# Inner seven-product multiplications for two of the seven up products of a mixture-of-experts kernel

## The chip, the cores and the metric

The kernel runs on one core of a Trainium2 chip. The metric is the device time of one execution in microseconds (us); lower is better. Before the change three runs took 1023.96, 1022.22 and 1023.16 us, a median of 1023.16.

## What is computed

Attention with feature maps makes x, of 4608 rows and 512 columns. Then every one of 8 experts is applied to all rows, and the results are added with weights P that come from a gate by eight rounds of row and column normalisation. Only the second part is touched:

```python
N, D, E, F = (4608, 512, 8, 1024)
...
for e in range(E):
    h = np.maximum(x @ w1[e], 0.0)
    ye = h @ w2[e]
    out += P[:, e:e + 1] * ye
```

## The kernel before

**Tiles.** The 4608 rows are 9 groups g of 512 rows. `xT` in SBUF holds x transposed, 512 features on four blocks of 128 partitions. Expert 0 runs on plain matmuls (L581) while the attention and the routing still use the other engines. Experts 1 to 7 use a multiplication of 2x2 blocks with seven products in place of eight (Strassen in Winograd's form): `sums_up` (L1201) makes sums of the blocks of w1 on VectorE, `sums_down` (L1226) those of w2, and `sums_x` (L1277) sums of the blocks of x, once, in expert 1; they are stored in DRAM (`Xd`) and loaded again by `load_x` (L1295) for each later expert.

**Stages.** Groups are worked in pairs (0,1), (2,3), (4,5), (6,7), and group 8 alone. For a pair there are two calls of `up7` (L1321), one for each half `fp` of the 1024 hidden columns; for group 8 there is one. Each call stands in one stage together with one `down7` (L1441) for one earlier group. So an expert has 4 x 2 + 1 = 9 stages, and the seven experts have 63. In experts 1 to 6 group 8 comes last, in expert 7 first.

**The up products.** In a pair's stage `up7` makes the seven products for two tiles q of 128 hidden columns. Each product for one q is two 512-column matmuls (`wide`, L1312, recorded at L1316), one for each 128 rows of its K of 256. So a stage has 7 x 2 x 2 = 28 of these. Their names are x1 (a block of w1 times a block of x, both as they are: product "11"), y1, x2, w1 (product "s1": a sum of w1 blocks times a sum of x blocks), x3, x4 and w2; x10 is x1 for q = 0. x1, x2, x3 and x4 add up in one PSUM bank per q. After x1, x2 and x3 ScalarE copies this running sum into an SBUF buffer U (`keep`, L1359), and VectorE adds U to the bank of y1, w1 or w2, clips at zero and writes the hidden tile `hs` (`add`, L1363, recorded at L1364). After x4 ScalarE applies Relu to the bank (`relu`, L1368).

**The down products.** `down7` has seven products X1, Y1, Z1, X2, X3, Z2, X4, each of eight 256-column matmuls (`product`, L1301, recorded at L1307), 56 in a stage. VectorE makes sums of the hidden tiles first (`sub`, L1199, 128x512 each). A product's bank is read into the accumulator `acc` either by VectorE (`read`, L1501) or, in `read2` (L1507), by two ScalarE reads scaled by P (L1513) and a POOL addition (L1516). Each of X1 and Y1 has such a `read2` into the same part of `acc`.

**Order.** All operations are recorded in a `Plan` (L192) first. A list scheduler with its own durations for each engine then writes them out: it always takes the operation that can start first, and among equals the one recorded first. For a stage, the order of recording is the string `ORDER` (L1566). PSUM has eight banks of 512 fp32 columns per partition, which `Banks` (L70) hands out one or two at a time. The rings T (sums of w1, 4 buffers), U (4) and X (sums of x, 4) are handed out in the same way. `sub` operations and POOL's operations are planned as sharing one port.

## Time and profile before

| | |
|---|---|
| median of three runs | 1023.16 us |
| span of the profiled execution, first to last instruction | 1020.7 us (no other time of this execution is given; the median lies 2.46 above it) |
| granted TensorE clock | 1.000 of full speed |
| matmul L1316, 128x512, and L1307, 128x256 | 379 ns and 273 ns each |
| ScalarE copy into U, L1360, 128x512 | 588 ns, x378 |
| ScalarE scaled read, L1513, 128x256 | 476 ns, x496 |
| ScalarE Relu, L1369, 128x512 | 609 ns, x126 |
| VectorE addition with clipping, L1364, 128x512 | 687 ns, x378 |
| POOL addition, L1516, 128x512 | 1309 ns, x248 |

The engines are PE (TensorE's matmuls), PEld (its weight loads), DVE (VectorE), ACT (ScalarE), POOL (GpSimd) and SP (which issues DMAs). A group's mean is the length of one instruction from its start to its end. Instructions of one engine overlap: of two that follow each other without a wait, the second starts before the first ends. So the time by which one instruction moves the next, its pace, is shorter than its length, and is read from rows of the timeline that merge several of them.

### The profile page before, as it was taken

What the parts mean: (1) busy time and instruction counts of PE and PEld (TensorE: products, weight loads), DVE (VectorE), ACT (ScalarE), POOL (GpSimd) and SP (SyncE); (2) the same over time, 40 slices, a digit from 0 to 9 for tenths busy, and PEclk for the clock granted to TensorE, in tenths of its full rate; (3) what the DMA queues carried; (4) which work ended last, traced back from release to release, by engine and by line L of the source; (5) the groups of instructions that cost most, each with busy time, mean ns of one, the idle gap of its engine ahead of it and who ended that gap; (6) DMA issues with size and microseconds to landing.
All of it is one profiled execution on the core that took longest, in us unless ns stands there. A gap on an engine that the chain in (4) does not pass through costs nothing.

```text
span 1020.7 us, 21372 instructions
## 1 busy us (share of the span) xinstructions
PE 1007.1 (99%) x7944; PEld 686.1 (67%) x7944; DVE 853.2 (84%) x1833; ACT 701.6 (69%) x1530; POOL 466.8 (46%) x480
## 2 busy tenths in 40 slices
PE   7899999999999999999999999999999999999998
PEld 5666666644566766676667766676667666776665
DVE  7999989987888987788778887788778877888776
ACT  7999999836778665666666666556666666655663
POOL 5778764400244444444444444544444444544443
PEclk9999999999999999999999999999999999999999
DMA  9999988160103311161106111421125110612333
GB/s 264 174 194 175 174 149 126 36 114 11 42 32 69 82 32 32 27 135 32 32 27 114 33 42 37 82 54 32 31 47 115 32 32 26 109 43 73 129 124 130
DMA packets 107016, 82.86 MB, mean 81 GB/s; under 512 B 53536, under 2 KB 89376, under 8 KB 106912
## 3 DMA queue, kind: packets, MB, share of 16 engines
q1 hardware_dynamic: 74960, 57.44, 22.4%
q0 software_dynamic: 31648, 23.86, 16.9%
q8 instruction: 62, 1.02, 0.4%
q14 instruction: 42, 0.34, 0.1%
q10 hardware_dynamic: 304, 0.20, 0.1%
HBM read 83.18 MB, written 12.98 MB: 94 GB/s over the span
## 4 chain that ended last, share of the span: by engine, by line
PE 95%; ACT 2%; DVE 1%; issue 0%; POOL 0%; DMA 0%; DVEq 0%; ACTq 0%
PE ps L1307 41%; PE ps L1316 33%; PE ps L581 18%; PE ps L864 2%; PE ps L711 0%; ACT q L577 0%; DVE m L573 0%; ACT k L577 0%; DVE wx L573 0%; DMA acc<-in_k_dram 0%; PE ps L893 0%; ACT kr L577 0%; ACT wx L577 0%; DVE xb L878 0%; PE ps L903 0%
## 5 line engine op out<-in xcount | busy, mean ns | idle before, releaser
L1516 POOL TENSOR_TENSOR acc<-acc,hx 128x512 f32<-128x512 f32 x248 | 322.9, 1309 | 476.7 <-ACT hx L1513 473.3
L1360 ACT COPY U<-ps 128x512 f32<-128x512 f32 x378 | 216.6, 588 | 134.1 <-PE ps L1316 117.6
L1513 ACT ACTIVATE hx<-ps,P 128x256 f32<-128x256 f32 x496 | 208.0, 476 | 124.6 <-PE ps L1307 112.0
L1364 DVE CUSTOM_DVE_ANT_0 hs<-ps,U 128x512 bf16<-128x512 f32 x378 | 253.0, 687 | 35.7 <-PE ps L1316 15.0
L1307 PEld LDWEIGHTS <-hs 128*128 128x128 bf16 x1984 | 194.1, 98 | 72.8 <-issue 0.2
L1501 DVE SCALAR_TENSOR_TENSOR acc<-ps,P,acc 128x256 f32<-128x256 f32 x372 | 161.2, 478 | 92.3 <-PE ps L1307 91.5
L1307 PEld LDWEIGHTS <-hx 128*128 128x128 bf16 x1488 | 145.6, 98 | 40.0 <-issue 0.2
L1307 PE MATMUL ps<-hx,hs 128*128 128x256 bf16 x992 | 132.5, 273 | 0.0
L1316 PE MATMUL ps<-X,T 128*128 128x512 bf16 x448 | 129.0, 379 | 0.3 <-ACT U L1360 0.2
L1316 PE MATMUL ps<-xT,wx 128*128 128x512 bf16 x384 | 101.5, 379 | 0.0
L1316 PEld LDWEIGHTS <-T 128*128 128x128 bf16 x672 | 65.8, 98 | 48.0 <-issue 0.3
L1369 ACT ACTIVATE hs<-ps 128x512 bf16<-128x512 f32 x126 | 73.2, 609 | 12.3 <-PE ps L1316 12.3
L1307 PE MATMUL ps<-wx,hs 128*128 128x256 bf16 x560 | 80.4, 273 | 0.0
L1316 PEld LDWEIGHTS <-wx 128*128 128x128 bf16 x512 | 50.1, 98 | 38.4 <-issue 0.5
L1316 PE MATMUL ps<-xT,w 128*128 128x512 bf16 x288 | 75.6, 379 | 0.0
L581 PE MATMUL ps<-w,hx 128*128 128x512 bf16 x288 | 73.7, 379 | 0.0
L581 PE MATMUL ps<-xT,w 128*128 128x512 bf16 x288 | 72.9, 379 | 0.0
L1307 PE MATMUL ps<-wx,hx 128*128 128x256 bf16 x496 | 68.4, 273 | 0.0
L1316 PE MATMUL ps<-xT,T 128*128 128x512 bf16 x224 | 66.0, 379 | 0.0
L1307 PE MATMUL ps<-hx 128*128 128x256 bf16 x496 | 64.3, 273 | 0.1
L1199 DVE TENSOR_TENSOR hx<-hx,hs 128x512 bf16<-128x512 bf16 x124 | 64.2, 518 | 0.0
L1307 PE MATMUL ps<-w,hs 128*128 128x256 bf16 x432 | 62.7, 273 | 0.0
(147 smaller groups left out, 1516.2 us busy)
## 6 DMA issues: line engine op xcount, KB each, us to landing
X<-xd SPq DMA_DIRECT2D x72, 256.0 KB, 2.6
wx<-in_moe_w_dram POOLq DMA_DIRECT2D x8, 1024.0 KB, 12.5
v_m<-in_v_dram SPq DMA_DIRECT2D x15, 512.0 KB, 5.3
out_dram<-acc SPq DMA_DIRECT2D x14, 512.0 KB, 2.8
w<-in_moe_w_dram POOLq DMA_DIRECT2D x6, 1024.0 KB, 12.0
qk<-in_k_dram POOLq DMA_DIRECT2D x12, 256.0 KB, 5.5
qk<-in_q_dram POOLq DMA_DIRECT2D x12, 256.0 KB, 6.3
xd<-X SPq DMA_DIRECT2D x12, 256.0 KB, 2.1
```

The lines of the kernel that those rows point to most:

```text
L581: nc.tensor.matmul(out_, lhsT=lhsT, rhs=rhs, start=start, stop=stop)
L864: pe(65, lambda j=j: nc.tensor.matmul(pn()[:, j * D1:j * D1 + D1], lhsT=s["T"][x]()[:, j % 2, 2 * h + j // 2, :] if j < 4 else r["T"][x]() ...
L1199: lambda: f.tensor_tensor(out=out_(), in0=x(), in1=y(), op=op), r, w, **kw)
L1307: pe(256, lambda i=i, k=k, z=z: nc.tensor.matmul(bank()[:, 256 * i:256 * i + 256], lhsT=lhs(k, i), rhs=rhs(k), start=first and z, stop=k = ...
L1316: pe(512, lambda k=k: nc.tensor.matmul(bank().rearrange("p (a b) -> p a b", a=2), lhsT=lhs(k), rhs=rhs(k), start=first and k == 0, stop=k ...
L1360: act(512, lambda: nc.scalar.copy(out=u[q][n]().rearrange("p a b -> p (a b)"), in_=x[q]()), [x[q]], [u[q][n]])
L1364: dve(515, lambda: nc.vector._custom_dve(ADD_SAT, out=out_(q, i, j), in0=bank[q]().rearrange("p (a b) -> p a b", a=2), in1=u[q][n](), s0=3 ...
L1369: act(512, lambda: nc.scalar.activation(out=out_(q, i, j), in_=x[q]().rearrange("p (a b) -> p a b", a=2), func=ACT.Relu, bias=0.0, scale=1 ...
L1501: dve(320, lambda n=n, ts=ts: nc.vector.scalar_tensor_tensor(out=acc[g][:, ts, 256 * j:256 * j + 256], in0=bank()[:, 256 * n:256 * n + 256 ...
L1513: act(370, lambda n=n: nc.scalar.activation(out=u()[:, n, :], in_=bank()[:, 256 * n:256 * n + 256], func=ACT.Copy, bias=0.0, scale=P[:, 4 ...
L1516: pool(695, lambda: nc.gpsimd.tensor_tensor(out=acc[g][:, 2 * i:2 * i + 2, 256 * j:256 * j + 256], in0=acc[g][:, 2 * i:2 * i + 2, 256 * j: ...
```

## The change

Four things change together.

- **Inner products.** In experts 2 to 7, for pairs of groups, the products "11" (x1) and "s1" (w1) are no longer four 512-column matmuls each for the two q. Each becomes seven products of half the size again, a chain of seven 256-column matmuls with K = 128, named ia1 to ia7 (for "11") and ib1 to ib7 (for "s1"). The running sums of these chains stay in PSUM: after the first product ScalarE copies half a bank into half of another bank, after the second it copies half a bank into a U buffer, and after the third and the fourth VectorE adds U and writes half a bank of PSUM. The fifth to seventh products then accumulate on these halves. `inner_sums` makes the four sums of w1 blocks for each chain in T (for expert 7 in the free w1 buffer). `inner_x` makes sums of x blocks during expert 1, three of which go to DRAM through a new ring XI of two buffers and are loaded for every pair of the later experts; the fourth overwrites a block of xT.
- **Running sums copied between banks.** In all seven experts, where x1's sum went into U and VectorE added it to y1's bank, ScalarE now copies it into y1's bank (`move`), y1 accumulates on it, and ScalarE applies Relu. x2's sum is copied in the same way into a bank for w2. w1's sum is kept in U and added at x3. So per q there are two additions by VectorE and two Relus in place of three and one. In `down7`, X1's sum is copied into Y1's bank by ScalarE, and only Y1 is read into `acc`.
- **Banks.** A bank on which matmuls accumulate after a copy (kind "onto") must have been written over its whole width before; `Banks` keeps the set `whole` of those.
- **Rings and order.** T has 5 buffers, U 3, X 3, XI 2. Stages with inner products are recorded in the new order `INNER`.

```diff
-    ring("s_p", [128, 1024], BF16, "T", 4)
-    ring("s_p", [128, 2, 256], FP32, "U", 4)
-    ring("s_p", [128, 2, 2, 256], BF16, "X", 4)
+    ring("s_p", [128, 1024], BF16, "T", 5)
+    ring("s_p", [128, 2, 256], FP32, "U", 3)
+    ring("s_p", [128, 2, 2, 256], BF16, "X", 3)
+    ring("s_p", [128, 3, 256], BF16, "XI", 2)
...
+    def inner_sums(w1, i, key, late, spare, at):
+        S = spare or new("T")
...
+        for n, x, y, op in ((3, b(0, 0), b(1, 0), ALU.subtract), (1, b(1, 0), b(1, 1), ALU.add),
+                            (2, c(1), b(0, 0), ALU.subtract), (4, b(0, 1), c(2), ALU.subtract)):
+            sub(dve, 256, c(n), x, y, op, k + late, [own])
...
+    def inner_x(gs, r0=()):
+        keys = xall(gs)
+        for n, j in INNER_X:
+            X = {n: new("XI")}
+            b = [[xpart(gs, j, k, a) for a in range(2)] for k in range(2)]
...
+            sub(dve, 256, t(3), b[1][1], b[0][1], ALU.subtract, keys + ["late", *r0], w)
+            sub(dve, 256, b[0][1], b[0][1], b[0][0], ALU.subtract, ["late", *r0], keys)
+            sub(dve, 256, t(2), b[1][1], b[0][1], ALU.subtract, keys + ["late", *r0], w)
+            sub(dve, 256, t(4), b[1][0], t(2), ALU.subtract, keys + ["late", *r0], w)
+            move_x(gs, n, True, X)
...
+        def move(to, q):
+            act(512, lambda: nc.scalar.copy(out=to[q](), in_=x[q]()), bk(x[q]), [to[q]])
...
+        def chain(name, o, r, takes, wk, posts):
...
+            def step(i):
+                if i == 1:
+                    one(1, 0, "11", "11", True)
+                    copy(at(0, 0), 0, k[0, 0])
+                elif i == 2:
+                    one(1, 1, "s1", "t1")
+                    copy(s, 1, (p5, n))
+                elif i == 3:
+                    one(1, 0, "s2", "t2")
+                    plus(0, 1)
+                elif i == 4:
+                    one(1, 0, "s3", "t3")
+                    plus(1, 1)
+                elif i == 5:
+                    one(0, 0, "12", "21")
+                elif i == 6:
+                    one(0, 1, "s4", "22")
+                    posts(0)
+                else:
+                    one(1, 0, "22", "t4")
+                    posts(1)
...
         def x1(q):
-            prod(x, q, "11", "11", True, more, u[q] + hb)
-            keep(q, 0)
+            prod(x, q, "11", "11", True, more, hb)
+            move(y, q)
 
         def y1(q):
-            prod(y, q, "12", "21", True, r0, hb)
-            add(y, q, 0, 1, 1)
+            prod(y, q, "12", "21", False, r0, hb)
+            relu(y, q, 1, 1)
 
         def x2(q):
             prod(x, q, "s2", "t2", False)
-            keep(q, 1)
+            move(z, q)
 
         def w1(q):
-            prod(w, q, "s1", "t1", True, A["s4"][1] + r0, hb, [("banks", q)])
+            prod(w, q, "s1", "t1", True, A["s4"][1] + r0, hb, [("banks", 0, q)])
+            keep(q)
 
         def x3(q):
             prod(x, q, "s3", "t3", False)
-            keep(q, 0)
-            add(w, q, 0, 0, 0)
+            add(x, q, 0, 0)
...
         def w2(q):
-            prod(w, q, "s4", "22", False)
-            add(w, q, 1, 1, 0)
+            prod(z, q, "s4", "22", False)
+            add(z, q, 1, 0)
...
         def X1():
             prod(x, a(0, 0), "11", hk(0, 0), True, sk(1) + hk(1, 0),
                  [("D", e, g)])
-            read2(x, 0, 0)
+            act(512, lambda: nc.scalar.copy(out=y(), in_=x()), [x], [y])
 
         def Y1():
-            prod(y, a(0, 1), "21", hk(0, 1), True, [("D", e, g)])
+            prod(y, a(0, 1), "21", hk(0, 1), False, [("D", e, g)])
             read2(y, 0, 0)
...
+    INNER = ("ib1 ia1 ia2 ib2 ib3 ia3 X1 Z1 ib5 ia4 ib4 ia5 ia6 ib6 y10 X2 x20 ia7 X3 x21 ib7 "
+        "x31 y11 w20 x30 Z2 x40 x41 Y1 X4 w21").split()
```

In the chain, `one(i, h, ...)` is the 256-column matmul into half h of bank i (bank 0 is the chain's result for q = 0, bank 1 for q = 1), `copy` is a 256-column ScalarE copy, `plus` a 256-column VectorE addition into PSUM, and `posts` is what followed x1 or w1 before: `move` into y's bank for "11", `keep` into U for "s1".

## The prediction

> **What bounds the kernel now.** I read the page's engine shares first, then the chain that ended last, then the busy time in windows inside the experts.

> ```profile
> span 1020.7 us, 21372 instructions
> ...
> PE 1007.1 (99%) x7944; PEld 686.1 (67%) x7944; DVE 853.2 (84%) x1833; ACT 701.6 (69%) x1530; POOL 466.8 (46%) x480
> ...
> PE 95%; ACT 2%; DVE 1%; issue 0%; POOL 0%; DMA 0%; DVEq 0%; ACTq 0%
> PE ps L1307 41%; PE ps L1316 33%; PE ps L581 18%; PE ps L864 2%; PE ps L711 0%; ACT q L577 0%; DVE m L573 0%; ACT k L577 0%; DVE wx L573 0%; DMA acc<-in_k_dram 0%; PE ps L893 0%; ACT kr L577 0%; ACT wx L577 0%; DVE xb L878 0%; PE ps L903 0%
> ```

> TensorE is busy for 99% of the span, and 95% of the last chain lies on it, 74% in L1307 and L1316, the products of experts 1 to 7. The window over the middle (columns: window, length, then busy us and count of PE, weight loads, DVE, ACT, POOL, then the granted clock, DMA share, GB/s):

> ```profile
> 514.00:621.00 107.00, 107.00 (x770) 75.06 (x768) 87.53 (x183) 66.24 (x140) 47.89 (x38) 1.00 0.24 54
> ```

> TensorE has no idle time here, at clock 1.00. Work taken off it is time won, and each wait put on it is time lost; nothing else can be won there. The chain in order of time shows one piece, 13.97 us of L1307, at 332.96, 442.51, 551.99, 661.47 and 770.95: 109.5 us for an expert, 12.17 for each of its 9 stages. That fixes the unit of what follows.

> **What leaves TensorE.** The timeline gives the pace of matmuls (start, us, engine, line, operation, shapes, count):

> ```profile
> 548.37 1.03 PE L1316 MATMUL ps<-X,T 128*128 128x512 bf16 x4
> ...
> 551.83 1.04 PE L1307 MATMUL ps<-hx,hs 128*128 128x256 bf16 x8
> ```

> One 512-wide matmul lasts 0.379 us in the groups, so the next starts (1.03 - 0.379)/3 = 0.217 later; I use 0.216. For 256 wide it is (1.04 - 0.273)/7 = 0.1095. A stage of 28 wide and 56 narrow ones is 28 x 0.216 + 56 x 0.1095 = 12.18, as measured. In each of the 48 changed stages (6 experts, 4 pairs, 2 halves) 8 wide ones become 14 narrow ones: 1.728 us become 1.533, so 0.195 less. **48 x 0.195 = 9.4 us.** The build agrees: 384 wide matmuls fewer, 672 narrow ones more. Their weight loads double per column, but L1307 keeps this pace with a 0.098 us load for each 0.1095 us matmul, so loads stay covered. Up to the last products of expert 0 the order on TensorE is the same; expert 1 has the same matmuls as before.

> **What is added on other engines, all beside TensorE.** ScalarE: of a stage's six 512-wide copies into U, four now write PSUM, at the same count; two Relus are added (0.52 each from pairs of L1369), four 256-wide copies in a changed stage, and in the down product one 512 copy (0.485, from pairs of L1360 that take 1.07) replaces two scaled reads (0.42 each). From 66.24/107 x 12.17 = 7.53 us per stage this makes 7.53 + 1.04 + 4 x 0.31 + 0.485 - 0.84 = 9.5 of 11.98. VectorE: two additions of L1364 leave (0.60 each), four 256-wide additions into PSUM come, and the sums of weights. L872 is their nearest row, VectorE from PSUM to PSUM with 325 elements at 495 ns, and TensorE accumulates on it afterwards; at L1364's slope (512 elements, 687 ns) 256 elements take about 0.42, paced 0.33. From 87.53/107 x 12.17 = 9.95 this makes 9.95 - 1.20 + 1.32 + 0.28 (eight weight sums over eight stages) = 10.35 of 11.98. POOL loses one 1.31 us addition a stage. The 48 weight sums (256 elements; 0.285 from the rows of 512 at 0.418 and 1024 at 0.685) and 32 sums of x are 23 us of VectorE, hidden under TensorE unless they stand in front of something it waits for (below). XI adds 8 stores and 48 loads of 192 KB on SP; each load is asked for when the previous pair's seventh inner product is done (4 to 5 us into its second stage) and needed 1.3 us or more into the next stage, 8 us later. X loads land in 2.6 us by the median and 7.3 at most. X with three buffers reloads each a stage ahead of use. I cost all of it at nothing; a pair whose load came without that cover would wait up to 2.6 us.

> **What waits are added.** Here lies the risk: each inner chain has three round trips, TensorE to ScalarE or VectorE and back, and what waits on TensorE holds everything behind it. I followed the build's order through a pair's two stages and through a change of expert, with three allowances. A narrow result is ready 0.20 us after the next matmul could start: 0.273 - 0.1095, and 0.04 until its reader starts (two matmuls end at 545.05, L1360 starts at 545.09). From an end to the waiting matmul I take 0.06 (L872 ends at 35.92, its matmul starts at 35.98). The rest are the paces above; times below count from the stage's first inner product. The tightest place is the start of a pair's second stage: the first products of both chains are readable at 0.53 us, and four 256 copies follow each other. No ScalarE write to PSUM and no plain 256 copy is in the trace. Nearest rows, both from PSUM to SBUF:

> ```profile
> 102.11 1.24 ACT L577 ACTIVATE kr<-ps 128x256 bf16<-128x256 f32 x4
> ```

> ```profile
> 548.20 0.84 ACT L1513 ACTIVATE hx<-ps,P 128x256 f32<-128x256 f32 x2 [0.47 <-PE ps L1307]
> ```

> Four Exps take 1.24 us, a pace of 0.27. The scaled copy paces 0.364 and lasts 0.476; it reads a scale per partition, which the new copy does not. By the first row the third and fourth copies end at 1.50 and 1.77 and TensorE may go on at 1.56 and 1.83; it arrives at the two third products at 1.64 and 1.86. No wait. By the second row they end at 1.73 and 2.10: 0.30 us lost by the fourth. I take the first, since like the new copy it reads no memory scale, and keep the second as an end. The next tightest there is ia7: VectorE has an addition at 2.31, subtractions at 2.66 and 3.04, and the addition that ia7 waits for from 3.45 to 3.87; go at 3.93, reached at 3.96. The other products have 0.03 to 0.1 to spare; nothing is late. In a pair's first stage two are late. Z1's bank is read until 1.05, go at 1.11, reached at 1.09: 0.02. For ib5 VectorE has w21's addition at 0.97, a subtraction at 1.57 and the addition from 1.90 to 2.33; go at 2.39, reached at 2.32: 0.07. After a change of expert five T buffers are refilled, the last four weight sums just before ib1; the build fills in with some 27 down matmuls, and only w20 is late (ScalarE's Relu at 4.87, the copy from 5.40 to 5.99, go at 6.05, reached at 6.00). That is 0 in half of the stages and 0.09 in the other half: 48 x 0.045 = **2.2 us lost**. The other end, the scaled copy's row in 24 second stages, is 24 x 0.30 = 7.2 more; below zero nothing is possible, since TensorE has no idle to give back.

> [...]

> **Sum.** The profiled execution spans 1020.7; the median of 1023.16 lies 2.46 above it, which I keep as what lies around the span (no other time of that execution is given). 1020.7 - 9.4 + 2.2 = 1013.5, and 1013.5 + 2.46 = **1016.0**.

> **Rivals.**
> 1. *The copies into PSUM are slower than the Exps.* For it: no row shows the operation, and ScalarE goes from 62% to 80% busy. Against: pace 0.27 of the nearest row. At L1513's price 1016.0 + 7.2 = 1023.2, no change; halfway about 1019.6.
> 2. *VectorE's queue becomes the bound, and it ends slower.* Fourth and seventh products wait for a 256 addition, and in the build a pair's second stage puts two L1199 subtractions right before one of them, with 0.03 to spare. L1199 can be held up by POOL:

> ```profile
> 547.81 2.68 POOL L1516 TENSOR_TENSOR acc<-acc,hx 128x512 f32<-128x512 f32 x2 [3.08 <-ACT hx L1513]
> ...
> 548.01 1.34 DVE L1199 TENSOR_TENSOR hx<-hx,hs 128x512 bf16<-128x512 bf16 x1
> ```

> 1.34 us in place of 0.42. Over all four forms the means are 518, 439, 421 and 418 ns: 124 x 124 ns = 15.4 us of such delay, 0.25 a stage. If it falls before an addition in every changed stage: 48 x 0.25 = 12 us, 1028.0. It decides from 9.4/48 = 0.196 us of waits per stage. Against: POOL has a quarter less to do, and in my walk the subtractions end before POOL starts.
> 3. *The change does not shorten TensorE's work*, because narrow matmuls pace at their weight loads. The L1307 row excludes it.

> **How the numbers follow.** A measurement of this kernel tells about 0.2% (2 us) from no change: 1021.1 to 1025.2 is "the same". The forecast, 1013 to 1019, has 0.62. Rival 1 has 0.21, spread over 1019 to 1025, 0.11 of it below 1021.1. Rival 2 has 0.13, 1025 to 1034, with 0.01 on the side of the same. Faster than 1013 or anything unnamed: 0.04, of which 0.02 is faster. So faster 0.75, the same 0.12, slower 0.13 (0.01 of the unnamed). The floor is the full gain, 1020.7 - 9.5 + 2.46 = 1013.7, less 0.9 for the spread of the three runs: 1012.8. Upwards, 1022.5 leaves out rival 2, the top of rival 1 and half of the unnamed, 0.19 in all.

> **What would show it.** TensorE's busy time falls to about 998 us. An expert from 2 to 6 takes 109.5 - 8 x 0.15 = 108.3 us. The 256 copies' pace is near 0.27, the 256 additions last near 0.42, and TensorE's waits for ScalarE and VectorE inside the experts total 1 to 4 us; if they are over 9 us, rival 1 or 2 holds, and the line named in the wait tells which. L1199's mean falls from 518. XI never appears as a releaser. I am wrong if a bank, a T buffer or XI, and not a copy or an addition, holds TensorE.

## The result and the profile after

The changed kernel takes **1027.68 us** (median of four runs, 1026.86 to 1029.21) against 1023.28 in the same comparison: a ratio of 1.0048 [1.0034, 1.0062]. It is slower, by about 0.5%; 1016.0 was forecast, in a range up to 1022.5. The profiled span went from 1020.7 to 1025.3, +4.6.

The page of the changed kernel, first lines and the chain that ended last:

```profile
span 1025.3 us, 22492 instructions
...
PE 1001.4 (98%) x8232; PEld 712.2 (69%) x8232; DVE 849.4 (83%) x1979; ACT 799.8 (78%) x1786; POOL 385.7 (38%) x418
...
PE 91%; DVE 5%; ACT 3%; DMA 1%; issue 1%; SPq 0%; DVEq 0%; ACTq 0%
```

TensorE is busy for 5.7 us less, but idle for 23.9 us where it was 13.6; VectorE's share of the last chain rose from 1% to 5%. The window over the middle, same columns as before:

```profile
514.00:621.00 107.00, 106.25 (x815) 79.43 (x814) 87.95 (x207) 81.25 (x181) 36.44 (x29) 1.00 0.31 69
```

VectorE's load is hardly other than before (87.53), POOL's fell from 47.89 to 36.44, the clock is 1.00. The same piece of an expert in the chain in order of time gives the length of an expert:

```profile
558.50 15.50 PE ps L1379 x142
...
667.84 15.50 PE ps L1379 x142
...
777.28 15.50 PE ps L1379 x142
```

109.34 and 109.44 us, before 109.5; 108.3 was forecast. What holds TensorE between 260 and 1010 us is in the view of its waits (who waited <- for whom: us, times, longest):

```profile
PE ps L1475 <- DVE ps L1487: 5.3, 8, 0.8
PE ps L1379 <- ACT hx L1656: 1.6, 2, 1.2
PE ps L1388 <- DVE hs L1450: 1.6, 3, 1.2
PE ps L1388 <- DMA X<-xd: 1.2, 1, 1.2
```

In the kernel before this view has one line, 0.2 us. It counts only idle time; a wait also takes the 0.16 us by which one narrow matmul otherwise starts before the other's end. So I also add up, over all pairs of successive matmuls, the time from start to start less the pace (0.216 us, narrow 0.1095). This **lateness** is the measure in the rest; the line numbers of after are L1475 (inner products), L1484 (their copies), L1487 (their additions), L1447 (copies between banks), L1450 (addition with clipping), L1211 (all sums), L1659 (POOL's addition).

| kernel | 255 to 340 us (expert 1) | 340 to 925 | 925 to the end | sum |
|---|---|---|---|---|
| before | 0.4 | -0.9 | -0.2 | -0.7 |
| after | 3.4 | 8.3 | 1.7 | 13.4 |

The sum of before is the error of the two paces. The difference, 14.1 us, less the 9.4 us by which the narrow matmuls are shorter, is 4.7: the span's 4.6. So the gain is there in full, and 14.1 us of waits stand against the 2.2 that were forecast. By place:

- **A, 4.6 us.** Five times 0.92 us, at 379.60, 489.02, 598.11, 707.63 and 816.89: the fifth inner product of a chain (ib5) waits for an addition, where the down products change from one expert to the next.
- **B, 3.0 us more than before in expert 1**, where the up products are those of before: waits of 1.36 and 0.60 for ScalarE, and one of 1.34 for VectorE (an x4, see runs 3 and 4).
- **C, 2.5 us** in the first inner products of expert 2 (354 to 360 us): five waits, three of them, 2.1 us, for additions (0.43, 0.79 and 0.84).
- **D, 1.4 us** in expert 7: X is not there.
- **The rest, 2.6 us**, in many waits of 0.4 us and less.

A, then the last two waits of C, then D in the timeline of after (start, length, engine, line, operation, then idle time and what ended it):

```profile
485.36 1.34 POOL L1659 TENSOR_TENSOR acc<-acc,hx 128x512 f32<-128x512 f32 x1 [3.10 <-ACT hx L1656]
...
485.49 1.75 DVE L1211 TENSOR_TENSOR hx<-wx,hx 128x1024 bf16<-128x1024 bf16 x1
...
487.17 0.86 DVE L1644 SCALAR_TENSOR_TENSOR acc<-ps,P,acc 128x256 f32<-128x256 f32 x2
...
487.96 0.67 DVE L1450 CUSTOM_DVE_ANT_0 hs<-ps,U 128x512 bf16<-128x512 f32 x1
...
488.56 0.41 DVE L1487 TENSOR_TENSOR ps<-ps,U 128x256 f32<-128x256 f32 x1
...
489.02 0.27 PE L1475 MATMUL ps<-xT,wx 128*128 128x256 bf16 x1 [0.76 <-DVE ps L1487]
```

```profile
357.69 0.27 PE L1475 MATMUL ps<-xT,w 128*128 128x256 bf16 x1
357.71 0.48 DVE L1644 SCALAR_TENSOR_TENSOR acc<-ps,P,acc 128x256 f32<-128x256 f32 x1 [1.17 <-PE ps L1379]
358.11 0.42 DVE L1487 TENSOR_TENSOR ps<-ps,U 128x256 f32<-128x256 f32 x1
358.58 0.27 PE L1475 MATMUL ps<-XI,T 128*128 128x256 bf16 x1 [0.63 <-DVE ps L1487]
...
359.64 0.27 PE L1475 MATMUL ps<-XI,w 128*128 128x256 bf16 x1 [0.68 <-DVE ps L1487]
```

```profile
935.79 6.22 SPq L1195 DMA_DIRECT2D out_dram<-acc  x8
942.11 1.02 SPq L1329 DMA_DIRECT2D X<-xd  x2
945.11 1.02 PE L1388 MATMUL ps<-X,T 128*128 128x512 bf16 x4 [1.19 <-DMA X<-xd]
```

Read A upwards from the matmul. It waits for the addition that ended at 488.97. Its operands were there at 487.07, when ib3 had ended; what came first was VectorE's queue, back to a sum of w2 blocks that took 1.75 us instead of 0.68. That sum started 0.13 us after an addition on POOL, and ended 0.54 us after it. It is the fourth sum of w2. In the kernel before, the fourth runs alone, in 0.68 us; there it is the third that starts beside POOL's addition and takes 1.49, six times, and TensorE is not late for anything behind it (lateness -0.9 between 340 and 925):

```profile
474.87 2.95 POOL L1516 TENSOR_TENSOR acc<-acc,hx 128x512 f32<-128x512 f32 x2 [3.08 <-ACT hx L1513]
475.19 1.49 DVE L1199 TENSOR_TENSOR hx<-wx 128x1024 bf16<-128x1024 bf16 x1
...
481.24 0.68 DVE L1199 TENSOR_TENSOR hx<-wx,hx 128x1024 bf16<-128x1024 bf16 x1
```

In C, VectorE had been idle for 1.17 us just before the last two waits, which are 1.6 of the 2.5 us, and the sums of w1 had ended at 353.4. What stands there is a read of a down product's bank ahead of the addition, and only two inner products between two waits. At the start of expert 3, where six down matmuls stand between (466.83 to 467.49), there is no wait. The 0.43 before that, at 355.81, does come behind the weight sums: from them on VectorE had no idle time.

In D, two of a pair's three X loads are asked for at 942.11, after eight output stores of group 8 that kept SP's queue for 6.22 us. Before, all three were asked for at 921.75, ahead of the stores; the fourth X buffer had made that possible.

### The profile page after: what moved, and what is told of

It reads as the page before. It is cut to its first block, busy times and chain, and to the rows that moved or that the text cites. A ratio compares the mean times of both kernels' runs of the same rounds, so it can differ in the third digit from the quotient of the medians.

```text
span 1025.3 us, 22492 instructions
## 1 busy us (share of the span) xinstructions
PE 1001.4 (98%) x8232; PEld 712.2 (69%) x8232; DVE 849.4 (83%) x1979; ACT 799.8 (78%) x1786; POOL 385.7 (38%) x418
## 3 DMA queue, kind: packets, MB, share of 16 engines
q8 instruction: 64, 1.05, 0.4%
## 4 chain that ended last, share of the span: by engine, by line
PE 91%; DVE 5%; ACT 3%; DMA 1%; issue 1%; SPq 0%; DVEq 0%; ACTq 0%
PE ps L1379 39%; PE ps L1388 24%; PE ps L593 18%; PE ps L1475 7%; PE ps L876 2%; DVE hx L1211 1%; DMA acc<-in_q_dram 1%; DVE hs L1450 1%; ACT k L589 1%; ACT q L589 1%; DVE acc L1644 1%; DVE m L585 0%; ACT hx L1656 0%; DVE hs L1211 0%; DVE wx L585 0%
## 5 line engine op out<-in xcount | busy, mean ns | idle before, releaser
L1659 POOL TENSOR_TENSOR acc<-acc,hx 128x512 f32<-128x512 f32 x186 | 241.9, 1301 | 562.4 <-ACT hx L1656 561.6
L1379 PEld LDWEIGHTS <-hs 128*128 128x128 bf16 x1984 | 193.7, 98 | 59.9 <-issue 2.6
L1450 DVE CUSTOM_DVE_ANT_0 hs<-ps,U 128x512 bf16<-128x512 f32 x252 | 164.7, 684 | 60.6 <-PE ps L1388 57.1
L1455 ACT ACTIVATE hs<-ps 128x512 bf16<-128x512 f32 x252 | 151.3, 606 | 57.4 <-PE ps L1388 51.6
L1656 ACT ACTIVATE hx<-ps,P 128x256 f32<-128x256 f32 x372 | 157.8, 479 | 38.5 <-PE ps L1379 34.2
L1379 PEld LDWEIGHTS <-hx 128*128 128x128 bf16 x1488 | 145.5, 98 | 30.5 <-issue 0.2
L1447 ACT COPY ps<-ps 128x512 f32<-128x512 f32 x252 | 146.8, 592 | 25.3 <-PE ps L1475 9.7
L1379 PE MATMUL ps<-hx,hs 128*128 128x256 bf16 x992 | 134.4, 272 | 1.9 <-ACT hx L1656 1.6
L1487 DVE TENSOR_TENSOR ps<-ps,U 128x256 f32<-128x256 f32 x192 | 76.0, 425 | 19.6 <-PE ps L1475 13.3
L1379 PE MATMUL ps<-wx,hs 128*128 128x256 bf16 x560 | 79.5, 273 | 0.0
L1443 ACT COPY U<-ps 128x512 f32<-128x512 f32 x126 | 74.8, 593 | 3.1 <-PE ps L1475 2.7
L1379 PE MATMUL ps<-wx,hx 128*128 128x256 bf16 x496 | 73.9, 273 | 0.0
L593 PE MATMUL ps<-xT,w 128*128 128x512 bf16 x288 | 72.9, 379 | 0.0
L1379 PE MATMUL ps<-hx 128*128 128x256 bf16 x496 | 70.5, 273 | 0.0
L1379 PE MATMUL ps<-w,hx 128*128 128x256 bf16 x432 | 66.5, 273 | 0.0
L1484 ACT COPY ps<-ps 128x256 f32<-128x256 f32 x96 | 32.1, 360 | 38.5 <-PE ps L1475 25.7
L585 DVE TENSOR_REDUCE m<-ps 128x4 f32<-128x512 f32 x88 | 58.7, 678 | 3.8 <-PE ps L593 2.0
```

The costliest lines, as they stand in the source:

```text
L593: nc.tensor.matmul(out_, lhsT=lhsT, rhs=rhs, start=start, stop=stop)
L1379: pe(256, lambda i=i, k=k, z=z: nc.tensor.matmul(bank()[:, 256 * i:256 * i + 256], lhsT=lhs(k, i), rhs=rhs(k), start=first and z, stop=k = ...
L1443: act(512, lambda: nc.scalar.copy(out=u[q]().rearrange("p a b -> p (a b)"), in_=w[q]()), bk(w[q]), [u[q]])
L1447: act(512, lambda: nc.scalar.copy(out=to[q](), in_=x[q]()), bk(x[q]), [to[q]])
L1450: dve(515, lambda: nc.vector._custom_dve(ADD_SAT, out=out_(q, i, j), in0=bank[q]().rearrange("p (a b) -> p a b", a=2), in1=u[q](), s0=3.0e ...
L1455: act(512, lambda: nc.scalar.activation(out=out_(q, i, j), in_=bank[q]().rearrange("p (a b) -> p a b", a=2), func=ACT.Relu, bias=0.0, scal ...
```

## The experiments

**Theory P** (formed from A): what is new is not that VectorE's sums are held by POOL, but that TensorE now waits for plain VectorE work that stands behind such a sum. **Rivals:** the order of the chains itself is too tight, held or not; the copies between banks are slow; the rings are too small. Each time is followed by its ratio to the kernel before, run beside it, with a 95% interval.

**1. POOL's additions made short.**

```diff
-                out=acc[g][:, 2 * i:2 * i + 2, 256 * j:256 * j + 256],
-                in0=acc[g][:, 2 * i:2 * i + 2, 256 * j:256 * j + 256], in1=u(), op=ALU.add),
+                out=acc[g][:, 2 * i:2 * i + 2, 256 * j:256 * j + 4],
+                in0=acc[g][:, 2 * i:2 * i + 2, 256 * j:256 * j + 4], in1=u()[:, :, 0:4], op=ALU.add),
```

> The changed kernel in the same order on every engine and with the same waits; only POOL's addition into acc covers 8 of its 512 elements per partition (the rest of those additions is left out), so POOL holds its port a fraction of the 1.3 us. Theory (POOL's port): the five waits of 0.92 us, one after each change of expert, go, and the wait of 1.34 us at 295 us, before which a sum of x took 1.35 us, goes too: 1027.7 - 4.6 - 1.3 = 1021.8, between 1021 and 1022.5. Rival (VectorE's queue is too full there by its order, with or without POOL): the five waits stay above 0.5 us each and the time is 1026.5 to 1028.

1021.79 us, 0.9992 [0.9982, 1.0001]; lateness 7.3 in place of 13.4. At the place of A:

```profile
482.75 0.28 POOL L1659 TENSOR_TENSOR acc<-acc,hx 128x8 f32<-128x8 f32 x1 [4.17 <-ACT hx L1656]
...
482.89 0.69 DVE L1211 TENSOR_TENSOR hx<-wx,hx 128x1024 bf16<-128x1024 bf16 x1
...
484.89 0.42 DVE L1487 TENSOR_TENSOR ps<-ps,U 128x256 f32<-128x256 f32 x1
```

The sum is back at 0.69, the addition comes 2.00 us after the sum's start and not 3.07, and all five waits are gone. Of B the wait of 1.34 fell to 0.28 (there a sum of x blocks had been held, 1.35 us); the other two, C and D stayed. P holds for some 6 us.

**2. The same by order alone.** In experts 1 to 5 the POOL addition of group 8's Y1 was recorded behind the sum.

> The changed kernel with one added wait: in the stage after a change of expert, the POOL addition of Y1 of group 8 waits until VectorE's last sum of w2 blocks is done, five times in all. Nothing else moves. Theory (POOL's port): that sum takes 0.68 us again, not 1.75, and the five waits of 0.92 us fall to under 0.1: 1027.7 - 4.5 = 1023.2, between 1022.5 and 1024. Rival (VectorE's queue too full by its order): at most 1 us is won, 1026.7 or more.

1027.99 us, 1.0054 [1.0039, 1.0069], all waits as they were. The lines say why: POOL still starts first.

```profile
485.44 1.35 POOL L1659 TENSOR_TENSOR acc<-acc,hx 128x512 f32<-128x512 f32 x1 [3.10 <-ACT hx L1656]
485.58 1.76 DVE L1211 TENSOR_TENSOR hx<-wx,hx 128x1024 bf16<-128x1024 bf16 x1
```

The order of recording binds only instructions of one engine; the two share no data, so nothing made POOL wait. The edit did not do what it was to do, and tells nothing on P.

**3 and 4. The copies between banks without the inner products**, with the new rings (3) and with those of before (4; the rings' lines of the diff are this run's alone):

```diff
-    INNER_W = [(n, i, i) for n, i in (("11", 1), ("s1", 0)) if n in ('11', 's1')]
+    INNER_W = [(n, i, i) for n, i in (("11", 1), ("s1", 0)) if n in ()]
...
-    INNER_X = [(n, j) for n, j in (("11", 1), ("s1", 0)) if n in ('11', 's1')]
+    INNER_X = [(n, j) for n, j in (("11", 1), ("s1", 0)) if n in ()]
...
-    ring("s_p", [128, 1024], BF16, "T", 5)
-    ring("s_p", [128, 2, 256], FP32, "U", 3)
-    ring("s_p", [128, 2, 2, 256], BF16, "X", 3)
-    ring("s_p", [128, 3, 256], BF16, "XI", 2)
+    ring("s_p", [128, 1024], BF16, "T", 4)
+    ring("s_p", [128, 2, 256], FP32, "U", 4)
+    ring("s_p", [128, 2, 2, 256], BF16, "X", 4)
+    ring("s_p", [128, 3, 256], BF16, "XI", 1)
```

> The changed kernel without inner products: all up products are whole ones again, in the order of recording of before; running sums are still copied between banks, and T, U and X keep the changed sizes (5, 3, 3). Theory (losses beside the chains): expert 1 keeps some 2 to 3 us of waits, and the load of X behind the stores of group 8 keeps 1.4, while the 9.4 us of matmuls and the waits of the chains both go: 1025.5 to 1028. Rival (the copies between banks and the ring sizes cost nothing; all the loss is the chains'): 1022.5 to 1023.8, as before.

> As the kernel without inner products, but with the ring sizes of before (T 4, U 4, X 4): copies between banks alone. Theory (X with three buffers is what costs in expert 1 and before the load of X): 1.5 to 3 us less than the kernel with X 3, 1023 to 1025, and no wait for a load of X near the end. Rival (the copies between banks themselves cost in expert 1): the same as with X 3 within 0.7 us.

1035.21 us, 1.0125 [1.011, 1.014], and 1032.89 us, 1.0099 [1.0082, 1.0115]: both outside what either side expected. Two things follow. The rings cost 2.3 us, and 2.0 of it lies in expert 1 (lateness there 2.6 with the new rings, 0.6 with the old): most of B. And the copies, costed at nothing, cost 10 us by themselves when the order of before is kept. Run 4 shows where, eleven times, twice in most experts:

```profile
477.94 2.63 POOL L1659 TENSOR_TENSOR acc<-acc,hx 128x512 f32<-128x512 f32 x2 [6.12 <-ACT hx L1656]
...
479.42 1.71 DVE L1211 TENSOR_TENSOR hx<-wx 128x1024 bf16<-128x1024 bf16 x1
...
481.05 1.28 DVE L1450 CUSTOM_DVE_ANT_0 hs<-ps,U 128x512 bf16<-128x512 f32 x2
481.78 0.59 PE L1388 MATMUL ps<-X,wx 128*128 128x512 bf16 x2 [0.84 <-DVE hs L1450]
```

x4 accumulates on x3's bank. Before, ScalarE copied that bank out and x4 went on; now VectorE's addition reads the bank itself, and x4 waits for VectorE, behind another held sum (here the third sum of w2, the one that was held before at no cost).

**5. The held sum moved.** The fourth sum of w2 is recorded behind the two additions of the third stage's "s1" chain, and waits for the second; on one engine, order binds.

```diff
-        sub(dve, 1024, t(3), q(*b21), t(1), ALU.subtract, k(b21) + [T[1]] + late, [T[3]])
+        def last(more=()):
+            sub(dve, 1024, t(3), q(*b21), t(1), ALU.subtract,
+                k(b21) + [T[1]] + late + list(more), [T[3]])
...
+                        if o == "ib4" and 1 < e < E - 1 and gs[0] == 2 and fp == 0:
+                            B7["last"]([("plus", 1, 1)])
```

> All work is kept. In experts 2 to 6 the fourth sum of w2 (128x1024, the one that a POOL addition stretched to 1.75 us at each change of down expert) stands in VectorE's queue behind the two additions of the first inner chain of the third stage, not ahead of them; nothing else is changed by hand. Theory (the sum held by POOL makes the addition late that step 5 of a chain waits for): the five waits of 0.92 us at 379.6, 489.0, 598.1, 707.6 and 816.9 go, 1027.7 - 4.6 = 1023.1, if the sum costs nothing at its new place (1022.5 to 1024). Rival (the addition is late there by the order of the chains itself, or the sum is held by the next POOL addition just as well): the waits stay or move, 1026.5 to 1028.5.

1022.32 us, 0.9996 [0.9986, 1.0005], 5.4 us less than the changed kernel: the theory's side, and a little more than its 4.6. One sum was moved at each of five changes of expert: it starts 5.20 us after POOL's addition and not 0.13. Same place (this kernel's lines stand four further on from L1379: L1383 to L1663 are L1379 to L1659):

```profile
484.97 1.34 POOL L1663 TENSOR_TENSOR acc<-acc,hx 128x512 f32<-128x512 f32 x1 [3.09 <-ACT hx L1660]
...
486.95 0.43 DVE L1491 TENSOR_TENSOR ps<-ps,U 128x256 f32<-128x256 f32 x1
...
487.43 0.27 PE L1479 MATMUL ps<-xT,wx 128*128 128x256 bf16 x1
...
490.17 0.68 DVE L1211 TENSOR_TENSOR hx<-wx,hx 128x1024 bf16<-128x1024 bf16 x1
```

**6 and 9. POOL's addition in two halves**, first as two operations that the scheduler places, then as two instructions in the place of the one, with every engine's order kept (the diff is the second's).

```diff
-            pool(695, lambda: nc.gpsimd.tensor_tensor(
-                out=acc[g][:, 2 * i:2 * i + 2, 256 * j:256 * j + 256],
-                in0=acc[g][:, 2 * i:2 * i + 2, 256 * j:256 * j + 256], in1=u(), op=ALU.add),
+            pool(695, lambda: [nc.gpsimd.tensor_tensor(
+                out=acc[g][:, 2 * i + n, 256 * j:256 * j + 256],
+                in0=acc[g][:, 2 * i + n, 256 * j:256 * j + 256], in1=u()[:, n, :], op=ALU.add)
+                for n in range(2)],
```

> All work is kept. Each POOL addition of 128x512 into acc is two of 128x256, each after its own ScalarE read, so twice as many POOL instructions. Theory (VectorE's sum is held until the POOL instruction that runs beside it ends): a hold costs about half, some 0.5 instead of 1.07 at the five changes of expert, so their waits fall from 0.92 to about 0.3 us and the time by about 3 us and some tenths for the other holds: 1023.5 to 1025.5. Rival (POOL's two halves follow each other without a gap, and VectorE is held until both have ended, or POOL's fixed time per instruction eats the gain): 1027 to 1029.

> As the run with POOL's additions in halves, but the two halves stand where the one addition stood, so that every engine's order is that of the changed kernel; all work is kept. Theory (a sum on VectorE is held until the one POOL instruction beside it ends, and may run before the next): the held sum of 128x1024 takes about 1.1 to 1.2 us in place of 1.75, the five waits fall from 0.92 to some 0.3 us, and the time to 1023.5 to 1025.5. Rival (the second half starts before VectorE gets its turn): the sum stays at 1.75 or more, 1027.5 to 1028.5. The 1042 of the other run is then the order's alone in both cases; if this run is over 1035 too, it is the halves themselves.

1042.26 us, 1.019 [1.0175, 1.0205], and 1037.63 us, 1.0145 [1.0129, 1.016]. Both are far above what either side expected. Run 9 shows the expected mechanism at the large sum, and a loss in place of the gain:

```profile
488.24 1.70 POOL L1659 TENSOR_TENSOR acc<-acc,hx 128x256 f32<-128x256 f32 x2 [2.81 <-ACT hx L1656]
488.41 0.95 DVE L1211 TENSOR_TENSOR hx<-hx,hs 128x512 bf16<-128x512 bf16 x1
489.28 1.21 DVE L1211 TENSOR_TENSOR hx<-wx,hx 128x1024 bf16<-128x1024 bf16 x1
```

A hold does end with the POOL instruction beside it: the large sum takes 1.21, not 1.75. But the subtraction ahead of it is now held by the first half, the sum by the second: the first half needs only the first of the two ScalarE reads and starts 0.17 us before that subtraction, where the whole addition started 0.20 us after it (485.36, against 485.16). Counting L1211 instructions over 0.12 us longer than usual: 52 with 25 us in all, against 12 with 9 us in the changed kernel. More holds, more of them ahead of what TensorE waits for: lateness 24.7. In run 6 the order differs as well, so it tells nothing more.

**7 and 8. Short POOL additions in run 4's kernel, and in the kernel before.** The edit of run 1.

> Copies between banks without inner products, with the rings of before (T 4, U 4, X 4), as the run at 1032.9; besides, each POOL addition covers 8 of its 512 columns, so its output lacks most of three of the down products' parts. Theory (the copies cost time only because x4 now waits for VectorE's addition, and that addition stands behind sums that POOL holds): the waits of 0.85 to 1.0 us twice in an expert go, 1032.9 - 8.5 = 1024.4 (1023 to 1026). Rival (x4 comes too soon after x3 for VectorE's addition, held or not): over 1030.

> The kernel before, with each POOL addition covering 8 of its 512 columns, so its output lacks most of those parts. Theory (before, no product of TensorE's near end waits for what stands behind a held sum; x4, y1 and w2 wait for ScalarE or have time): no change, 1022.3 to 1023.3, though its sums get shorter. Rival (the same holds cost the kernel before as much as the changed one, 5.9 us): 1017 to 1018.

1023.28 us, 1.0006 [0.9997, 1.0016], lateness -0.4: the eleven waits are gone, so the 10 us of the copies were held sums in front of x4's addition. And 1022.81 us, 0.9997 [0.9988, 1.0007]: the kernel before loses nothing to POOL, though 28 of its L1199 instructions are held, for 20 us in all, more than in the changed one. So P stands: held sums are old (which ones are held has shifted), a product that waits behind one is new. Runs 1 and 7 also give what the inner products, with their rings and their order, bring when nothing is held: 1023.28 - 1021.79 = 1.5 us, about the 9.4 less their 7.7 of lateness (7.3 + 0.4).

**10 to 12. Repairs.** Group 8's stores asked for by POOL (10); this, the moved sum, and no inner products for the first pair of expert 2 (11); only this and the moved sum (12). The second part of the diff is run 11's alone.

```diff
-                dma("SP", 1 << 17, 320, lambda b=b, rows=rows: nc.sync.dma_start(
+                dma("POOL", 1 << 17, 320, lambda b=b, rows=rows: nc.gpsimd.dma_start(
...
-                un = up7(A7, gs, fp, X, H, ["up0"])
+                un = up7({**A7, "inner": {}} if e == 2 and gs[0] == 0 else A7, gs, fp, X, H, ["up0"])
```

> The changed kernel, but group 8's eight stores in the last expert are asked for by POOL, no more by SP; all work is kept. Theory (the X loads of the next pair stand behind these stores on SP's queue, and TensorE waits 1.36 us for them): that wait goes or shrinks to the wait for the buffer, 1027.7 - 1.3 = 1026.4 (1026 to 1027.3). Rival (the third X buffer comes free that late, the stores are not what holds the loads): 1027.3 to 1028.2.

> Three repairs together, all work kept: the fourth sum of w2 behind the chain's additions (1022.3 alone), group 8's stores asked for by POOL, and no inner products for the first pair of expert 2, whose first stage had 2.5 us of waits. Theory: 1022.3 - 0.85 (the wait for X that is left there) - 2.5 + 2 x 0.195 + some waits that stay in the plain stage: 1019.5 to 1021, faster than both kernels by 0.2 to 0.3%. Rival (the waits of expert 2's start are VectorE's load after expert 1, and move on to the next pair): 1021.3 to 1023.

> Two repairs, all work kept: the fourth sum of w2 behind the chain's additions, and group 8's stores asked for by POOL. Theory (the two waits are independent): 1022.3 - 0.85 = 1021.4 (1020.8 to 1022), ahead of the kernel before by about 0.1%, and the 6 us of waits in expert 1 and at the start of expert 2 stay. Rival (the stores asked for by POOL take the port from VectorE, or the loads then wait for their buffer): 1022.0 to 1023.

Run 10: 1026.8 us, 1.0039 [1.0025, 1.0053]; the wait for X is gone, its lateness after 925 us is 0.3 in place of 1.7. Run 11: 1020.0 us, 0.9975 [0.9965, 0.9985]. Other than its expectation says, not all of its work is the reference's: the plain products of that pair read a block of x that `inner_x` has overwritten. As a time it tells that leaving out the inner products there wins C only in part: 0.6 us of waits stay in that stage, and x4 waits 1.01 us and an inner product 0.33 later on. Run 12 keeps everything: **1021.26 us, 0.9986 [0.9976, 0.9995]**, ahead of both kernels. Its remaining waits:

```profile
PE ps L1383 <- ACT hx L1660: 1.6, 2, 1.2
PE ps L1392 <- DVE hs L1454: 1.6, 3, 1.2
PE ps L1479 <- DVE ps L1491: 1.6, 3, 0.7
```

The lateness of all (the trace of run 12 lacks 37 matmul records; three gaps of 0.21 to 0.22 us in its row, 0.65 in all, are records that are missing and no waits):

| kernel | expert 1 | 340 to 925 | to the end | sum | us |
|---|---|---|---|---|---|
| 1 short POOL | 2.3 | 3.5 | 1.4 | 7.3 | 1021.8 |
| 2 order of recording | 3.4 | 8.9 | 1.3 | 13.6 | 1028.0 |
| 3 no inner products | 2.6 | 7.9 | 0.8 | 11.3 | 1035.2 |
| 4 the same, old rings | 0.6 | 8.6 | -0.2 | 9.0 | 1032.9 |
| 7 as 4, short POOL | 0.6 | -0.8 | -0.2 | -0.4 | 1023.3 |
| 5 sum moved | 3.4 | 3.4 | 1.2 | 8.0 | 1022.3 |
| 6 POOL in halves, other order | 2.6 | 22.6 | 3.3 | 28.6 | 1042.3 |
| 8 before, short POOL | 0.4 | -0.9 | -0.2 | -0.7 | 1022.8 |
| 9 POOL in halves | 3.8 | 17.0 | 3.9 | 24.7 | 1037.6 |
| 10 stores on POOL | 3.4 | 8.4 | 0.3 | 12.1 | 1026.8 |
| 11 three repairs | 3.4 | 2.8 | 0.0 | 6.2 | 1020.0 |
| 12 two repairs | 3.6 | 3.7 | 0.8 | 8.1 | 1021.3 |

## Why the prediction was wrong, point by point

- **What bounds the kernel, and the 9.4 us:** right. The new matmuls start 0.11 us apart (489.13, 489.24, 489.35, 489.46), and lateness less 9.4 gives the measured difference of the span. The 2.46 us taken for what lies around the span was a little large: in the four runs of the changed kernel time and span differ by 2.06 to 2.11.
- **Rival 1, slow copies into PSUM:** no. Two copies start 0.27 us apart (488.12 and 488.39), the pace that was taken, though each lasts 0.36 to 0.39: they overlap. The rows of the new operations:

```profile
L1447 ACT COPY ps<-ps 128x512 f32<-128x512 f32 x252 | 146.8, 592 | 25.3 <-PE ps L1475 9.7
...
L1487 DVE TENSOR_TENSOR ps<-ps,U 128x256 f32<-128x256 f32 x192 | 76.0, 425 | 19.6 <-PE ps L1475 13.3
...
L1484 ACT COPY ps<-ps 128x256 f32<-128x256 f32 x96 | 32.1, 360 | 38.5 <-PE ps L1475 25.7
```

 The additions last 0.425 (0.42 was estimated). Copies of 512 columns take no longer into PSUM than into SBUF: 592 ns against 593 (L1443) in the mean, where both mix copies that follow another instruction closely with copies that do not. Of the copies that found ScalarE idle, 80 into PSUM took 570 ns and 12 into SBUF 585.
- **"2.2 us lost", the step that failed.** 14.1 us came. For the steady stages the sum was about right: without A to D 2.6 us are left, though about 1.1 of it is x4's wait for VectorE (below), which the walk did not have, so a part of the agreement is luck. What failed is the sentence on the change of expert ("the build fills in with some 27 down matmuls, and only w20 is late"). It takes in the change of the up products, with their weight sums. A lies two stages later, where the down products change and sums of w2 go through VectorE's queue. That is a pair's first stage, for which the walk has ib5 late by 0.07 behind an addition and a subtraction; the prediction has no word on a sum of w2 ahead of them, and 0.92 came, in five stages. That such a sum can be held was to be read in the trace of before (the third one, 1.49 us, six times); that the fourth would be held was not, it took 0.68 there. That is A, 4.6 us.
- **"Expert 1 has the same matmuls as before":** true, and not enough. Smaller rings and the sums of x cost 3.0 us there (B; 2.0 by runs 3 and 4 from the rings; 1.06 less in run 1, where no sum of x is held).
- **"I cost all of it at nothing"** failed for three of its items, in whole or in part. X with three buffers cannot be loaded ahead of group 8's stores (D, 1.4). The start of expert 2 (C, 2.5) is not like that of later experts: the weight sums stand ahead of its first late addition, and further on too few products stand between an addition and the one that waits for it. The copies between banks, priced as ScalarE's time alone, move x4's wait from ScalarE to VectorE, 10 us with the old order (run 4); the new order puts other products between x3 and x4 and leaves about 1.1 of it (expert 1 keeps the old order, and the 1.34 of B is such a wait). The prediction names that wait nowhere.
- **Rival 2** had the right mechanism and the right side at 0.13. Its place was wrong (subtractions before ia7 in each second stage; it was a weight sum, five times), and so was its price: an average of the holds, 0.25 us a stage. Holds have no price by themselves: 20 us of them cost nothing before, 9 us cost some 6 after. The argument against it, that POOL has less to do, was beside the point for the same reason. L1199's mean did fall, from 518 to 433 ns for that form, while the kernel got slower.
- **What was to show it:** the test on TensorE's waits for ScalarE and VectorE (1 to 4 us forecast, over 9 for a rival) comes to 8.5 in the view, 6.9 of it for VectorE. It was built on idle time, which leaves out the first 0.16 us of each wait; so was the 998 us of busy time, of which 1001.4 came. XI was never a releaser, as forecast; X was.

Left open: which of the rings U, X and T makes B was not tried apart. What makes C is read from the trace and was not tested alone.

## What to carry to other kernels

When a change makes the critical engine wait for an engine that had slack, follow that engine's whole queue at the irregular places (a change of expert, the first pass, the last), and take each duration ahead of the waited-for instruction as it occurs there in the trace, not its mean. Delays that cost nothing today are listed in the trace already; what a change can do is to move them and to put something behind them. And when it has cost something, look for the one instruction to move before shortening all of them: five sums moved gave back 5 us, all additions in halves cost 10.
